# A bank of the score pool for the first of a tile's four transposed halves

## The chip, the cores and the metric

The kernel runs on one core of one Trainium2 chip. The metric is the device time of one execution in microseconds (us); three executions of the kernel before took 832.18, 831.68 and 832.12, median 832.12. One more execution was taken by the hardware profiler, and every row below is from it.

## The reference

Three stages follow one another. The change touches the first alone.

```
attention: B=2, H=8, S=768, D=64
  scores = q @ k.T / 8 + bias(head, distance)
  keep   = the first 8 keys, and the 96 latest keys up to the query itself
  a      = softmax(where(keep, scores, -1e9));  x = a @ v        -> 1536 x 512
experts (4): out += p[:, e] * (relu(x @ w1[e]) @ w2[e])
gate:        ((x @ w1) * (x @ w2)) @ w3 @ w_out
```

## The kernel before

The 1536 queries are cut into 12 tiles of 128 (6 for each batch). A loop of 12 turns, here turn 0 to turn 11, computes a tile's attention over a window of 232 keys (96 before, 8 global, 128 of its own; the first tile of a batch, in turns 0 and 1, has only its own 128). The eight heads are handled as two groups of four (`gr` 0 and 1). The order of all instructions on each engine is the order in which the code issues them. It is a software pipeline over three tiles; in the turn of tile `u`, `one_back` is the tile before it and `two_back` the one before that. The steps of a tile:

- scores (line 246, TensorE, called PE in the profile): per group two PSUM tiles `sp` from the pool `ps_s`, which has 4 banks. Per turn that is 8 matmuls in the program, 16 in the trace.
- `least` (line 261, VectorE, DVE): adds the bias and takes the negated row maximum, once per head, so 8 per turn; it is what frees a bank of the scores. A small read of the accumulator follows each.
- `weights` (line 272, ScalarE, ACT): the exponentials and their sums, 8 per turn.
- `inverse_sums` (lines 231, 232, DVE) and `normalize` (line 300, GpSimd, POOL): the weights are multiplied by the inverse of the sums, a run of four products per group.
- `transposes` (line 284, PE): each group of four heads is transposed in two halves, each half (two heads, two blocks of 128 each) into a PSUM tile `tp` from the pool `ps_t`, which has 3 banks. Four halves per tile of queries.
- `copy` (line 291): brings a half to SBUF as `ptT`. Half 0 of a group goes by DVE, half 1 by ACT.
- `values` (lines 323, 324, 326, PE): the product with v, into the one bank `op`, from which `split_x_hi` (line 444, ACT) and `split_x_lo` (line 450, DVE) write the two parts of x.

In a turn the PE does: the scores of `u`, the values of `two_back`, then the four halves of `one_back` (group 0 half 0, group 0 half 1, group 1 half 0, group 1 half 1). The copies of group 0 stand in the same turn, half 1 (ACT, between two exponentials) ahead of half 0 (DVE, behind the eight `least`); those of group 1 stand at the start of the next turn, behind the next scores. With three banks for four halves a turn, the fourth half takes the bank of the half whose copy stands first, group 0 half 1. From turn 6 on, ACT also casts a piece of the first expert's weights in each turn (line 340), and POOL subtracts it (line 341).

Behind the loop a tail finishes the last two tiles between the first matmuls of the experts (`up_ahead`, lines 56 to 58), and the experts and the gate follow, three matmuls for each product.

Of the kernel before, what the change touches and what calls it, by code (L numbers as in the profile page):

```python
# [8 lines left out]
F32 = mybir.dt.float32  # L9
# [9 lines left out]
P = 128  # L19
# [98 lines left out]
def banded_attention(tc, g, x_hi, x_lo, slots, experts):  # L118
    nc = tc.nc
    with ExitStack() as ctx:  # L120
# [7 lines left out]
        ps_s = ctx.enter_context(tc.tile_pool(name="ps_s", bufs=4, space=PSUM))  # L128
        ps_t = ctx.enter_context(tc.tile_pool(name="ps_t", bufs=3, space=PSUM))
# [146 lines left out]
        def transposes(u, gr):  # L276
            pt = st[u][gr]
            tps = []
            for half in range(2):
                tp = ps_t.tile([P, 2, 2, P], F32, name="tp")  # L280
                for hh in range(2):
                    for j in range(2 if u % NQ else 1):
                        c = slice(j * (LW + GW), j * (LW + GW) + P)
                        nc.tensor.transpose(tp[:, hh, j], pt[:, 2 * half + hh, c], g.ident)  # L284
                tps.append(tp)
            st[u][gr] = tps
# [57 lines left out]
        for m, u in enumerate(order):  # L344
# [39 lines left out]
            if m:  # L384
                transposes(one_back, 0)
                for half in (1, 0):
                    copy(one_back, 0, half)
# [11 lines left out]
            if m:  # L399
                transposes(one_back, 1)  # L400
# [11 lines left out]
        for gr in range(2):  # L412
            transposes(last, gr)
            if gr == 0:
                split_x_hi(nc, *outputs(prior))
            for half in range(2):
                copy(last, gr, half)
            if gr == 0:
                split_x_lo(nc, *outputs(prior))
# [878 lines left out]
```

## Time and profile before

| | |
|---|---|
| median of three runs | 832.12 us |
| the profiled execution, its time | 831.56 us |
| its span, first to last instruction | 829.6 us |
| PE busy | 812.8 us (98%), 4003 matmuls |
| DVE / POOL / ACT busy | 504.0 / 316.4 / 284.9 us |
| loop of 12 turns, first scores to the end of the last turn's transposes | 5.71 to 74.6 us |
| granted TensorE clock, mean | 0.998 |

PE is busy nearly throughout, so a whole-span share tells little: what matters is in which stretch PE's idle time lies, and what ended it. Busy time of matmuls is that of overlapping instructions with modelled ends, so the starts are the firmer numbers.

### The profile page before, as it was taken

How to read it: one execution, taken by the hardware profiler on the slowest of the kernel's cores; microseconds unless marked ns; L12 is line 12 of the kernel's file. 1: busy time of each engine (PE TensorE's matmuls, PEld its weight loads, DVE VectorE, ACT ScalarE, POOL GpSimd, SP SyncE). 2: the span in 40 equal slices, each digit the busy share in tenths (PEclk: the TensorE clock that was granted, in tenths of full speed). 3: DMA queues.
4: the chain of work that ended last, by engine and by line, in shares of the span. 5: the costliest groups of instructions: out<-in, count | busy, mean ns of one | idle time of the engine just before them, and what ended most of it. 6: DMA issues, size and time to landing. Idle time of an engine off the chain costs nothing.

```text
span 829.6 us, 11024 instructions
## 1 busy us (share of the span) xinstructions
PE 812.8 (98%) x4003; PEld 669.0 (81%) x4003; DVE 504.0 (61%) x945; ACT 284.9 (34%) x593; POOL 316.4 (38%) x318
## 2 busy tenths in 40 slices
PE   7999999999999999999999999999999999999997
PEld 4778888888888888888888888888788888888875
DVE  6886355557755556778738563665533743887840
ACT  6897321124321214333323321332442332333210
POOL 6686123535356455550344341422380003333300
PEclk9999999999999999999999999999999999999999
DMA  8850242557453556743101101110622210201011
GB/s 265 244 155 12 78 144 86 166 170 245 154 160 109 166 165 216 229 142 108 54 26 52 39 26 64 50 65 30 192 98 93 85 51 25 102 26 52 0 51 55
DMA packets 38132, 88.10 MB, mean 106 GB/s; under 512 B 3690, under 2 KB 9882, under 8 KB 38070
## 3 DMA queue, kind: packets, MB, share of 16 engines
q1 hardware_dynamic: 37398, 86.79, 32.9%
q8 instruction: 33, 0.54, 0.3%
q10 hardware_dynamic: 672, 0.54, 0.3%
q14 instruction: 29, 0.24, 0.1%
HBM read 73.66 MB, written 13.66 MB: 105 GB/s over the span
## 4 chain that ended last, share of the span: by engine, by line
PE 91%; DVE 4%; ACT 3%; DMA 1%; issue 1%; POOL 0%; DVEq 0%; ACTq 0%; POOLq 0%
PE z L56 18%; PE z L58 18%; PE z L57 18%; PE o L56 11%; PE o L58 11%; PE o L57 11%; DVE t L261 2%; ACT pt L272 2%; PE sp L246 1%; PE tp L284 1%; DMA keys<-in_k_dram 1%; ACT xh L444 1%; ACT ptT L291 0%; PE sp L56 0%; PE sp L58 0%
## 5 line engine op out<-in xcount | busy, mean ns | idle before, releaser
L58 PE MATMUL z<-xh,sl 128*128 128x512 f32 x428 | 166.6, 389 | 0.0
L56 PE MATMUL z<-xh,sh 128*128 128x512 f32 x428 | 166.5, 389 | 0.0
L57 PE MATMUL z<-xl,sh 128*128 128x512 f32 x428 | 166.5, 389 | 0.0
L547 POOL TENSOR_TENSOR cr<-cr,cb 128x512 f32<-128x512 f32 x40 | 51.6, 1290 | 126.6 <-issue 118.7
L58 PEld LDWEIGHTS z<-xh,sl 128*128 128x128 f32 x428 | 80.3, 188 | 17.2 <-DVE sl L51 0.2
L57 PEld LDWEIGHTS z<-xl,sh 128*128 128x128 f32 x428 | 80.3, 188 | 16.7
L56 PEld LDWEIGHTS z<-xh,sh 128*128 128x128 f32 x428 | 80.4, 188 | 16.6
L51 POOL TENSOR_TENSOR sl<-wr,sh 128x512 fp32r<-128x512 f32 (+1 forms) x32 | 32.1, 1024 | 148.7 <-ACT sh L50 148.4
L51 DVE TENSOR_TENSOR sl<-wr,sh 128x1024 fp32r<-128x1024 f32 (+1 forms) x57 | 70.3, 1240 | 23.5 <-ACT sh L50 22.7
L801 POOL TENSOR_TENSOR acc<-acc,t 128x512 f32<-128x512 f32 x36 | 49.3, 1403 | 85.1 <-DVE t L800 85.1
L50 ACT CAST sh<-wr 128x1024 fp32r<-128x1024 f32 (+2 forms) x89 | 70.6, 816 | 21.6 <-PE z L57 10.3
L532 POOL TENSOR_SCALAR ca<-ca 128x512 f32<-128x512 f32 x40 | 61.9, 1548 | 26.7 <-ACT ca L530 26.7
L700 DVE TENSOR_TENSOR t<-t,z 128x512 f32<-128x512 f32 x56 | 37.5, 681 | 32.3 <-PE z L58 27.9
L300 POOL TENSOR_TENSOR pt<-pt,r 128x232 f32<-128x232 f32 (+1 forms) x95 | 48.8, 546 | 16.3 <-ACT pt L272 9.6
L56 PE MATMUL z<-sh,sh 128*128 128x512 f32 x128 | 49.9, 390 | 0.8 <-DVE t L800 0.8
L57 PE MATMUL z<-sl,sh 128*128 128x512 f32 x128 | 49.8, 389 | 0.0
L58 PE MATMUL z<-sh,sl 128*128 128x512 f32 x128 | 49.8, 389 | 0.0
L272 ACT ACTIVATE pt<-t,negmax 128x232 f32<-128x232 f32 (+1 forms) x96 | 44.5, 465 | 10.1 <-DVE negmax L261 6.0
L261 DVE CUSTOM_DVE_ANT_0 t<-sp,bias 128x232 f32<-128x232 f32 (+1 forms) x96 | 30.5, 374 | 9.5 <-PE sp L246 9.5
L51 POOL TENSOR_TENSOR sl<-t,sh 128x256 fp32r<-128x256 f32 (+1 forms) x24 | 23.5, 995 | 31.3 <-ACT sh L50 31.1
L56 PE MATMUL o<-h0h,sh 128*128 128x512 f32 x84 | 32.8, 390 | 0.0
L57 PE MATMUL o<-h0l,sh 128*128 128x512 f32 x84 | 32.7, 389 | 0.0
(255 smaller groups left out, 1728.5 us busy)
## 6 DMA issues: line engine op xcount, KB each, us to landing
wr<-in_w_moe_dram SPq DMA_DIRECT2D x44, 512.0 KB, 4.2
raw<-in_w3t_dram SPq DMA_DIRECT2D x16, 512.0 KB, 4.7
raw<-in_w_ab_dram SPq DMA_DIRECT2D x16, 512.0 KB, 4.2
wr<-wab_d SPq DMA_DIRECT2D x16, 512.0 KB, 3.2
raw<-in_w_out_dram SPq DMA_DIRECT2D x8, 512.0 KB, 3.5
w3t_d<-cr SPq DMA_DIRECT2D x16, 256.0 KB, 2.4
wab_d<-cr SPq DMA_DIRECT2D x16, 256.0 KB, 2.2
wr<-w3t_d SPq DMA_DIRECT2D x8, 512.0 KB, 3.3
```

The costliest lines, as they stand in the source:

```text
L50: nc.scalar.copy(hi, src)
L51: (lo_engine or nc.vector).tensor_tensor(lo, src, hi.bitcast(F32), op=ALU.subtract)
L56: nc.tensor.matmul(out, wh, xh, start=start, stop=False)
L57: nc.tensor.matmul(out, wh, xl, start=False, stop=False)
L58: nc.tensor.matmul(out, wl, xh, start=False, stop=stop)
L261: nc.vector.tensor_tensor_reduce(out=t[:, 0:w], in0=st[u]["sp", gr][hh % 2][:, hh // 2, 0:w], in1=bb, scale=-SCALE, scalar=3.0e38, op0=ALU ...
L272: nc.scalar.activation(st[u][gr][:, hh, 0:w], t[:, 0:w], AF.Exp, bias=nm, scale=-1.0, accum_out=st[u]["sums"][:, h : h + 1])
L300: nc.gpsimd.tensor_tensor(pt[:, hh, 0:w], pt[:, hh, 0:w], r[:, hh : hh + 1].to_broadcast([P, w]), op=ALU.mult)
L532: nc.gpsimd.tensor_scalar(a, a, 2.0**-15, None, op0=ALU.max)
L547: nc.gpsimd.tensor_tensor(rest, rest, top.bitcast(F32), op=ALU.add)
L700: add = lambda o, a, b: nc.vector.tensor_tensor(o, a, b, op=ALU.add)
L801: nc.gpsimd.tensor_tensor(acc[c][:, d], acc[c][:, d], t, op=ALU.add)
```

## The change

The tile of group 0, half 0 comes from the pool of the scores, `ps_s`, under their name `sp`; the other three halves stay in `ps_t`, where each then has a bank of its own in every turn. Neither pool grows. The code is called from the same place, and nothing else is edited.

```diff
             for half in range(2):
-                tp = ps_t.tile([P, 2, 2, P], F32, name="tp")
+                first = gr == half == 0
+                tp = (ps_s if first else ps_t).tile([P, 2, 2, P], F32, name="sp" if first else "tp")
                 for hh in range(2):
```

The order of the instructions is the same on every engine; only waits of PE differ. The pool of scores now has five tiles in a turn for four banks, and hands a bank out in the order in which banks come free: the transposed half takes the bank of group 0's first score tile (free after the third `least`), and the next turn's four score tiles take those free after the fourth, the seventh and the eighth `least` and, last, the bank of the transposed half (free after its DVE copy).

The first place is PE in turn 4, before: the four halves `tp_576`, `tp_581`, `tp_599`, `tp_604`, and the score tiles of turn 5, `sp_618` to `sp_628`. In brackets stand the semaphores waited for.

```order
L284 MATMUL tp_576<-ident_63,pt_418 128x128 [waits Pool_49]
...
L284 MATMUL tp_581<-ident_63,pt_418 128x128 [waits PE_49,Pool_49]
...
L284 MATMUL tp_599<-ident_63,pt_425 128x128 [waits Pool_49]
...
L284 MATMUL tp_604<-ident_63,pt_425 128x128 [waits Activation_49,Pool_49]
...
L246 MATMUL sp_618<-keys_96,qr_403 128x232 [waits DMAHW2_49,DMAHW1_49,DVE_49]
```

The fourth half waits for ACT: the copy of the second half, whose bank it takes.

The same rows of the changed kernel, where the first half is `sp_576`:

```order
L285 MATMUL sp_576<-ident_63,pt_418 128x128 [waits DVE_49,Pool_49]
...
L285 MATMUL tp_581<-ident_63,pt_418 128x128 [waits PE_49,Pool_49]
...
L285 MATMUL tp_599<-ident_63,pt_425 128x128 [waits PE_49,Pool_49]
...
L285 MATMUL tp_604<-ident_63,pt_425 128x128 [waits Pool_49]
...
L246 MATMUL sp_618<-keys_96,qr_403 128x232 [waits DMAHW2_49,DMAHW1_49,DVE_49]
```

The wait for ACT is gone from the fourth half, and the first half waits for DVE instead. The third waits for PE itself, that is for its own bank's writes of the turn before.

The second place is PE's values in turn 4, which read the copied halves of the tile two back: before, the second half (`ptT_478`), the third and the fourth.

```order
L323 MATMUL op_557<-ptT_478,va_234 64x128
...
L323 MATMUL op_557<-ptT_526,va_234 64x128 [waits DVE_49]
...
L323 MATMUL op_557<-ptT_528,va_234 64x128 [waits Activation_49]
```

And now:

```order
L324 MATMUL op_557<-ptT_478,va_234 64x128 [waits Activation_49]
...
L324 MATMUL op_557<-ptT_526,va_234 64x128 [waits DVE_49]
...
L324 MATMUL op_557<-ptT_528,va_234 64x128 [waits Activation_49]
```

The wait for the ACT copy of the second half has moved here from the fourth half, to a matmul of the next turn.

## Rows read from the trace of the kernel before

**Rows 1.** Stretches: length, busy us (instructions) of PE, PEld, DVE, ACT, POOL, clock, DMA.
```profile
31.53:74.60 43.07, 40.55 (x449) 34.75 (x449) 34.68 (x161) 39.02 (x140) 34.34 (x62) 1.00 0.46 136
89.20:300.00 210.80, 210.80 (x932) 174.08 (x930) 120.91 (x204) 52.39 (x82) 86.54 (x63) 1.00 0.49 153
```
**Rows 2.** Groups by form, first 150 us: busy us, mean ns, idle before and releasers.
```profile
L284 PE MATMUL tp<-ident,pt 128*128 128x128 f32 x176 | 24.7, 279 | 7.1 <-ACT ptT L291 3.9 <-POOL pt L300 3.2
```
**Rows 3.** Chain that ended last, in turn 7: start us, us, what.
```profile
48.90 0.48 ACT ptT L291
...
49.51 0.63 PE tp L284 x4
```
**Rows 4.** Timeline of PE, turns 4, 7, 11: start us, us, what [idle before].
```profile
30.97 0.63 PE L284 MATMUL tp<-ident,pt 128*128 128x128 f32 x4 [0.36 <-ACT ptT L291]
...
43.89 1.84 PE L246 MATMUL sp<-keys,qr 64*128 64x232 f32 x16
...
47.62 1.53 PE L284 MATMUL tp<-ident,pt 128*128 128x128 f32 x12
49.51 0.63 PE L284 MATMUL tp<-ident,pt 128*128 128x128 f32 x4 [0.36 <-ACT ptT L291]
50.07 1.84 PE L246 MATMUL sp<-keys,qr 64*128 64x232 f32 x16
...
74.23 0.63 PE L284 MATMUL tp<-ident,pt 128*128 128x128 f32 x4 [0.36 <-ACT ptT L291]
```
**Rows 5.** Timeline of DVE, ACT, POOL, turns 7 and 8, and the tail.
```profile
45.48 0.49 ACT L272 ACTIVATE pt<-t,negmax 128x232 f32<-128x232 f32 x1 [0.54 <-POOL pt L300]
...
46.16 2.17 POOL L300 TENSOR_TENSOR pt<-pt,r 128x232 f32<-128x232 f32 x4 [0.71 <-ACT pt L272]
...
46.20 0.08 DVE L261 DVE_READ_ACCUMULATOR2_ANT negmax<- 128x1 f32 x1
...
48.31 0.69 DVE L291 COPY ptT<-tp 128x512 f32<-128x512 f32 x1 [0.43 <-PE tp L284]
...
49.46 2.17 POOL L300 TENSOR_TENSOR pt<-pt,r 128x232 f32<-128x232 f32 x4 [0.43 <-ACT ptT L291]
...
49.78 0.68 DVE L291 COPY ptT<-tp 128x512 f32<-128x512 f32 x1
...
50.71 0.41 ACT L340 CAST sh<-wr 128x256 fp32r<-128x256 f32 x1
51.15 0.40 DVE L261 CUSTOM_DVE_ANT_0 t<-sp,bias 128x232 f32<-128x232 f32 x1 [0.69 <-PE sp L246]
...
74.18 3.80 POOL L300 TENSOR_TENSOR pt<-pt,r 128x232 f32<-128x232 f32 x7 [0.44 <-ACT ptT L291]
```
**Rows 6.** Timeline of POOL, PE and DVE, turns 1 to 4.
```profile
9.30 2.97 POOL L300 TENSOR_TENSOR pt<-pt,r 128x128 f32<-128x128 f32 x8 [0.55 <-ACT pt L272]
...
13.30 1.84 PE L246 MATMUL sp<-keys,qr 64*128 64x232 f32 x16
...
15.66 1.47 POOL L300 TENSOR_TENSOR pt<-pt,r 128x128 f32<-128x128 f32 x4 [1.53 <-ACT pt L272]
...
18.19 2.17 POOL L300 TENSOR_TENSOR pt<-pt,r 128x232 f32<-128x232 f32 x4 [1.06 <-DVE r L232]
...
18.59 0.41 DVE L291 COPY ptT<-tp 128x256 f32<-128x256 f32 x1
...
19.17 1.84 PE L246 MATMUL sp<-keys,qr 64*128 64x232 f32 x16
...
20.25 0.40 DVE L261 CUSTOM_DVE_ANT_0 t<-sp,bias 128x232 f32<-128x232 f32 x1 [1.26 <-PE sp L246]
...
21.44 2.17 POOL L300 TENSOR_TENSOR pt<-pt,r 128x232 f32<-128x232 f32 x4 [1.08 <-ACT pt L272]
...
25.35 1.84 PE L246 MATMUL sp<-keys,qr 64*128 64x232 f32 x16
```
**Rows 7.** Timeline of PE, the last tile's transposes in the tail.
```profile
79.54 2.16 PE L284 MATMUL tp<-ident,pt 128*128 128x128 f32 x16
```

## The prediction

> **What bounds the kernel now.** I read the busy time by stretches first. From 89.2 to 300 us PE is busy for all of 210.80 us, at a granted clock of 1.00: the experts are bound by PE alone, and whatever starts them earlier ends the kernel earlier by as much. In the steady part of the attention loop, 31.53 to 74.60 us (seven turns), PE is busy for 40.55 of 43.07 us, also at 1.00 [rows 1]. So 2.5 us are idle there, seven times 0.36.
>
> The groups say what it is: the transposes wait 7.1 us in the loop, 3.9 of it for `ptT` of ACT and 3.2 put down to `pt` of POOL [rows 2]. The chain that ended last has the same link: the ACT copy 48.90 + 0.48 = 49.38, then the last four transposes at 49.51, a hand-over of 0.13 [rows 3]. The timeline of PE shows the place: twelve transposes at 47.62, then a stop of 0.36, then four, then the next turn's scores at 50.07. The same stop ends turn 4 at 30.97 and turn 11 at 74.23, eight times in all [rows 4]. A turn lasts 50.07 - 43.89 = 6.18 us.
>
> The stop costs more than its idle column says. Twelve transposes last 1.53 us and one 0.279 [rows 2, 4], so they start (1.53 - 0.279) / 11 = 0.114 us apart, the thirteenth could have started at 47.62 + 12 x 0.114 = 48.98, and it starts at 49.51: **0.53 us**. The Trainium skill ("Perfetto Trace Analysis", section "Identifying the Most-Contended Engine") says that matmul busy time measures badly because matmuls are pipelined; by the idle column the eight stops would be worth 8 x 0.36 = 2.9 us, by starts 8 x 0.53 = 4.2. I go by the starts.
>
> **The change, part by part.** *The wait removed in turns 4 to 11.* The fourth half's bank is free since the turn before, so it follows the third at once, if its weights are normalised: POOL's run of four ends at 46.16 + 2.17 = 48.33 [rows 5], 0.65 ahead of 48.98. PE then needs 6.18 - 0.53 = 5.65 us a turn. Whether the others can follow:
> - ACT goes from its first exponential at 45.48 to the end of its cast at 50.71 + 0.41 = 51.12, so 5.64 us, with no idle row between.
> - DVE: the copy of the first half starts 48.31 - 43.89 = 4.42 after the scores, the second copy ends 49.78 + 0.68 - 48.31 = 2.15 later, and the next `least` is due 51.15 - 50.07 = 1.08 after the next scores. The turn can't be shorter than 4.42 + 2.15 - 1.08 = 5.49.
> - POOL: the second run ends 49.46 + 2.17 - 43.89 = 7.74 after the scores, the first of the next turn is due 46.16 - 43.89 = 2.27 after its scores: 5.47 [rows 4, 5].
>
> All four fit in 5.65, with PE the last by a hair. Eight turns: 8 x 0.53 = 4.24 us.
>
> *Turns 1 to 3.* Here the same wait goes, and POOL is late next. A scores start follows the last transposes by 50.07 - 49.51 - 3 x 0.114 = 0.22.
> - Turn 1: POOL's products end at 9.30 + 2.97 = 12.27, the last transpose starts 0.13 later, turn 2's scores at 12.62 instead of 13.30: 0.68.
> - Turn 2: its products end at 15.66 + 1.47 - 0.68 = 16.45, so turn 3's scores start at 16.45 + 0.13 + 0.22 = 16.80 instead of 19.17: 2.37 by now. (The groups put 3.2 us of the transposes' idle time down to POOL. In this turn POOL's fourth product ended at 17.13, 2 us ahead of the scores, so it was another engine that PE waited for, and what the last transposes waited for besides is the ACT copy.)
> - Turn 3: DVE is behind now. Its second copy ends at 18.59 + 0.41 - 0.68 = 18.32, later than 16.80 + 1.08, so the first `least` moves from 20.25 to 18.32. POOL's second run would move with it from 21.44 to 19.51 but its first run ends at 18.19 + 2.17 - 0.68 = 19.68; from there 2.17 to 21.85. The last two transposes start 0.13 later, the scores 0.22 + 0.11 behind that: 22.31 instead of 25.35 [rows 6].
>
> So 3.04 us by turn 4. This part isn't shown as directly: it is at least the 0.68 of turn 1, at most 3.04. I take 3.04, because each step ends at a row.
>
> *Tail.* The last tile's 16 transposes take 2.16 us; unbroken they would take 0.279 + 15 x 0.114 = 1.99 [rows 2, 7]: 0.17.
>
> *Waits added.* The first half waits for the third `least`, whose read ends at 46.20 + 0.08, 1.34 before the transposes at 47.62 [rows 4, 5]. Behind it in PE's queue stand all other transposes and the next scores, so its cover matters: gone, it would cost its lateness in each turn. The next scores wait for `least` four, seven and eight and for the first half's copy, which ends at 48.31 + 0.69 = 49.00, against 49.54 for the first scores of the shorter turn, and the fourth bank is written later still. The wait in the values for the ACT copy comes a turn after that copy. All at nothing. The wait instruction itself, one more ahead of the first transposes, is not shown; its nearest row is the twelve transposes, with such a wait inside them and no gap: zero. The other end: as much as the hand-over of 0.13 in each of 11 turns, 1.4 us. Below nothing it can't be, since PE gains nothing by an instruction more.
>
> Sum: 4.24 + 3.04 + 0.17 = 7.45 us. The profiled execution, 831.56 (a span of 829.6 and 2.0 around it), becomes 824.1. The median of the runs is 0.56 above it, so **824.7 us** there.
>
> **Rivals.**
> 1. *Another engine becomes the bound, and a part is given back.* For it: ACT's 5.64 is within 0.01 of PE's 5.65, DVE and POOL within 0.2, and in turns 3 to 5 DVE and ACT are behind PE. Against: in turns 4 and 5 ACT has no cast. Should the turn stop at 5.9, the sum is 8 x 0.28 + 3.04 + 0.17 = 5.45, 826.7; should only turn 1 gain early on, 4.24 + 0.68 + 0.17 = 5.1, 827.0; both 3.1, 829.0. One way to it would be DVE and POOL slowing each other as they overlap more. The rows speak against: four products take 2.17 between DVE's instructions, 0.543 each, and seven take 3.80 in the tail, also 0.543 [rows 5]. The Trainium skill ("SBUF — State Buffer", section "Who interferes with whom") has a price for it where a DVE instruction reads two inputs from SBUF while GpSimd reads it; the trace shows none here.
> 2. *The change doesn't do what it says for the time:* the fourth half still starts at 49.51 for another reason that ends there, and nothing moves: 832.1. For it speaks that the idle row before the exponentials and those of the transposes name POOL too; against it, that POOL's products are over at 48.33.
> 3. *Slower: the DVE copy holds the scores.* Their fourth bank is now freed by a copy that DVE does behind eight `least`. It decides once the copy ends later than that bank is wanted: in the turn of 6.18 that is 50.07 + 10 x 0.115 (ten of the sixteen matmuls of 1.84 us) = 51.2, 2.2 after 49.00. Were the copy 2.5 late, each of 11 turns would cost 0.3 more than before: 835.4. Nothing in the rows makes it so late; the loop had 0.43 of idle right before it [rows 5].
>
> **How the numbers follow.** My forecast (6 to 8.5 us gained) 0.62; rival 1 (2 to 6 us) 0.28; no change 0.06; slower 0.04. 0.2% of 832 is 1.7 us, about what a measurement can tell from nothing. Faster is the first two, 0.90; same 0.06; slower 0.04. The likeliest case alone spans 823.6 to 826.1; to leave out no more than 2 in 10 the range takes in rival 1 down to 3.9 us, so 823.6 to 828.2.
>
> **What would show it.** Right: in turns 4 to 11 sixteen transposes without a stop, and scores that start 5.65 us apart; turn 4's scores near 22.3 and the last turn's transposes over near 67.2 instead of 74.6; the experts' stretch moved as a whole and no longer. If the turns are at 5.8 or more, the row of what PE waits for names the engine of rival 1; if PE stops ahead of its first transposes or its scores, for DVE, it is rival 3. Wrong altogether: an unchanged stop of 0.36 before the fourth half.

## The result and the profile after

The changed kernel's median is 824.66 us (823.10 to 825.47, six executions) against 831.79 for the kernel before in the same call: a ratio of 0.9911, 95% interval 0.9898 to 0.9924. It is faster, and 824.7 was forecast. Of all executions below one, with ten warm-up matmuls, took 1019.99 us at a mean granted clock of 0.753, and it is left out.

In the steady turns the stop before the fourth half [rows 4] is gone. The timeline of PE of the changed kernel, from turn 8 on (start us, us, what), with all lines one further down in the code:

```profile
46.40 1.84 PE L246 MATMUL sp<-keys,qr 64*128 64x232 f32 x16
...
50.13 0.66 PE L285 MATMUL sp<-ident,pt 128*128 128x128 f32 x4
50.62 1.47 PE L285 MATMUL tp<-ident,pt 128*128 128x128 f32 x12
52.02 1.84 PE L246 MATMUL sp<-keys,qr 64*128 64x232 f32 x16
```

The sixteen transposes run without an idle row, now as four under the scores' name and twelve under their own. A turn lasts 52.02 - 46.40 = 5.62 to 5.63 us instead of 6.18. The transposes start 50.13 - 46.40 = 3.73 after the scores, and before it was 47.62 - 43.89 = 3.73 too [rows 4]: the wait for `least` that now stands ahead of them costs nothing.

The stretches of it show the same (length, busy us and instructions of PE, PEld, DVE, ACT, POOL, clock, DMA); the first runs from turn 5's scores to the first matmul of `up_ahead` and answers to the first of [rows 1], the second is the experts':

```profile
29.52:68.73 39.21, 39.21 (x449) 34.89 (x449) 36.09 (x162) 39.16 (x141) 34.42 (x62) 1.00 0.52 155
83.06:300.00 216.94, 216.94 (x959) 179.32 (x958) 123.94 (x209) 52.85 (x83) 91.65 (x67) 1.00 0.49 156
```

PE was idle for 2.5 us there and is never idle now. ACT is busy for 39.16 of 39.21 us as well, which says by itself that one of the two is the bound and not which; an experiment below tells them apart.

The groups of the transposes in the first 150 us (busy us, mean ns, idle before), which answer to [rows 2]:

```profile
L285 PE MATMUL tp<-ident,pt 128*128 128x128 f32 x132 | 17.5, 276 | 0.2
L285 PE MATMUL sp<-ident,pt 128*128 128x128 f32 x44 | 7.3, 286 | 0.3 <-DVE negmax L261 0.3
```

and what PE waited for between 5 and 90 us (us, times, longest):

```profile
PE sp L246 <- DMA keys<-in_k_dram: 0.8, 1, 0.8
PE sp L285 <- DVE negmax L261: 0.3, 1, 0.3
PE op L327 <- ACT ptT L292: 0.2, 1, 0.2
```

Of 7.1 us of idle time ahead of the transposes 0.5 is left, and the new wait for DVE shows once, in turn 3.

Where the time came from, by starts on PE. One execution of each kernel is a thin base here, because the very beginning differs from one execution to the next; a later profile of the changed kernel began nearly as the one of before did, and stands in the last column. (One between the two, of 825.32 us, began late as well: turn 1's scores at 9.74, then 13.52, 44.85 and 14.31 for the next three rows.)

| stretch | before | changed | gain forecast | changed, later profile |
|---|---|---|---|---|
| start to turn 1's scores | 8.20 | 10.22 | 0 | 7.96 |
| turn 1 to turn 4 | 17.15 | 13.67 | 3.04 | 14.01 |
| turn 4 to the first `up_ahead` | 49.26 | 44.84 | 4.24 | 44.84 |
| from there to the experts' first `o` | 14.56 | 14.33 | 0.17 | 14.32 |
| the rest of the span | 740.43 | 740.44 | 0 | 739.77 |

The change is worth 3.14 + 4.42 + 0.24 = **7.80 us** for nearly the same start (forecast 7.45). In the first profile 1.7 of it are missing: turn 1 began 2.02 later, and turns 1 to 3, 0.34 shorter than in the later profile, gave that much back. The last row says nothing about the change: in the fourteen profiles of this case, of all kernels, the rest of the span lies between 739.5 and 741.1 us, the changed kernel's among them at 740.44, 740.88 and 739.77.

### The profile page after: what moved, and what is told of

It is laid out like the page before. It is cut to its first block, busy times and chain, and to the rows that moved or that the text cites. A ratio compares the mean times of both kernels' runs of the same rounds, so it can differ in the third digit from the quotient of the medians.

```text
span 823.5 us, 11032 instructions
## 1 busy us (share of the span) xinstructions
PE 813.5 (99%) x4002; PEld 670.3 (81%) x4003; DVE 505.1 (61%) x945; ACT 283.9 (34%) x593; POOL 316.4 (38%) x318
## 4 chain that ended last, share of the span: by engine, by line
PE 96%; ACT 1%; DVE 1%; DMA 1%; issue 0%; POOL 0%; ACTq 0%; DVEq 0%
PE z L56 18%; PE z L57 18%; PE z L58 18%; PE o L58 11%; PE o L56 11%; PE o L57 11%; PE sp L246 2%; PE tp L285 1%; PE op L324 1%; PE op L325 1%; ACT pt L272 1%; PE sp L285 1%; DMA keys<-in_k_dram 1%; PE sp L56 0%; PE sp L58 0%
```

## The experiments

All were timed beside the kernel before. Its medians in the four calls were 830.95, 832.18, 832.18 and 831.48, so each ratio counts against its own call, and the stretches of the profiles carry what is below 1 us.

**Is it the number of banks?** The changed kernel with one bank fewer for the transposes, so the other three halves share two:

```diff
-        ps_t = ctx.enter_context(tc.tile_pool(name="ps_t", bufs=3, space=PSUM))
+        ps_t = ctx.enter_context(tc.tile_pool(name="ps_t", bufs=2, space=PSUM))
```

> The changed kernel, but the pool of the transposed halves has two banks in place of three; the first half still lies in a bank of the scores, and the order is the same. The fourth half of a turn then takes the bank of the second half again and waits for its ACT copy, as in the kernel before. Theory (that one wait is what costs): everything else of the change is there, yet the stop before the fourth half is back in turns 1 to 11, a turn lasts 6.18 us, and the time is that of before, 831.8 +- 0.7. Rival (the gain comes from the scores' and halves' other banks or from the fifth tile in the pool of scores, not from this wait): turns of 5.63, about 824.7.

832.22 us, ratio 1.001 (0.9999 to 1.002). The stop is back; PE's timeline of this kernel:

```profile
47.41 0.66 PE L285 MATMUL sp<-ident,pt 128*128 128x128 f32 x4
47.90 1.04 PE L285 MATMUL tp<-ident,pt 128*128 128x128 f32 x8
49.30 0.63 PE L285 MATMUL tp<-ident,pt 128*128 128x128 f32 x4 [0.36 <-ACT ptT L292]
49.86 1.84 PE L246 MATMUL sp<-keys,qr 64*128 64x232 f32 x16
```

A turn is 6.18 again (43.68 to 49.86). The whole gain is thus that the fourth half doesn't take a bank that ACT's copy must first empty; that the first half lies in another pool gives nothing by itself.

**Are the terms separate?** The change in turns 1 to 3 alone, and in turns 4 to 11 and the tail alone:

```diff
-                first = gr == half == 0
+                first = share and gr == half == 0
...
-                transposes(one_back, 0)
+                transposes(one_back, 0, m < 4)
```

> The change in turns 1 to 3 alone; from turn 4 on and in the tail all four halves lie in the three banks as before. Theory: the turns from 4 on last 6.18 us again, and what is gained is the early part, which my working put at 3.04 and the profile of the changed kernel shows as 1.46 at turn 4's scores with a start that came 2.0 later: 2.5 to 3.5 us by the clock of equal starts, 828.3 to 829.3. Rival (only turn 1's 0.68 is gained, the rest is lost to POOL and DVE): 831.1.

> The change in turns 4 to 11 and in the tail alone; turns 1 to 3 as before. Theory: eight turns at 5.63 in place of 6.18 and the tail's 0.2: 4.4 + 0.2 = 4.6 us, 827.2. By the idle column of the trace of before (eight stops of 0.36) it would be 2.9 + 0.2, 828.7. Rival (another engine takes over as soon as the turns get short, and the early lead is what hides it): turns of 5.8 or more, 828.5 to 830.

Turns 1 to 3 alone: 828.19 us, ratio 0.9963 (0.9950 to 0.9977). Turns 4 to 11 and the tail: 827.78, ratio 0.9956 (0.9942 to 0.9970); its six times lie in two groups, 826.48 to 827.03 and 828.54 to 828.73, on either side of the 827.2 expected, so the stretches of the profile say more than this median. In the profile of the first, turn 1 to turn 4 takes 13.99 instead of 17.15, a gain of 3.16. But turn 4 then lasts 6.74 (PE, and ACT's copy of the second half):

```profile
22.01 1.84 PE L246 MATMUL sp<-keys,qr 64*128 64x232 f32 x16
25.74 1.53 PE L285 MATMUL tp<-ident,pt 128*128 128x128 f32 x12
27.46 0.58 ACT L292 COPY ptT<-tp 128x512 f32<-128x512 f32 x1
28.19 0.63 PE L285 MATMUL tp<-ident,pt 128*128 128x128 f32 x4 [0.92 <-POOL pt L301]
28.75 1.84 PE L246 MATMUL sp<-keys,qr 64*128 64x232 f32 x16
```

With the shared bank ACT's copy is waited for again, and ACT is behind by then: its copy runs at 27.46 for 0.58, and the fourth half starts 0.15 behind it (the row names POOL, whose products of that half were long done). So 0.57 of the 3.16 is given back where the bank is shared, and none where it isn't. In the profile of the second, turn 4 to `up_ahead` takes 44.84 and the tail 14.33, gains of 4.42 and 0.23, as with the whole change. Apart the two gain 2.59 + 4.65 = 7.24, together 7.80, and the difference is what turn 4 gave back.

**The changed kernel again.**

> The changed kernel once more, unchanged, for a second profile and more times. Theory: 824.7 again; the profile of the first look had its first matmuls 0.457 us apart up to 10.2 us, where the profile of before had 0.245 from 6.8 us on, so turn 1 started at 10.22 in place of 8.20 there. If that is chance, a second look may show turn 1 at 8.2, turn 4 near 22.3 and a time near 823; times spread over 2 us. If the change causes it, the second look has the late start as well.

> The changed kernel once more, beside the next one in the same call: 822.9 to 825.5, both paces of the start among its runs, median near 823.5 to 824.5.

823.18 us (ratio 0.9898, 0.9882 to 0.9913) and 824.67 us (0.9913, 0.9900 to 0.9926). Of 15 executions of this kernel seven lie between 822.88 and 823.47 and eight between 824.48 and 825.47, nothing between. The rows of the beginning tell the two apart. The changed kernel's first profile (825.47 us):

```profile
5.54 2.08 PE L246 MATMUL sp<-keys,qr 64*128 64x128 f32 x16 [0.78 <-DMA keys<-in_k_dram]
7.55 2.74 PE L172 MATMUL tp<-warm 128*128 128x512 bf16 x6
10.22 1.30 PE L246 MATMUL sp<-keys,qr 64*128 64x128 f32 x16
```

and the later one (822.92 us), with POOL's products of turn 3:

```profile
5.47 1.16 PE L246 MATMUL sp<-keys,qr 64*128 64x128 f32 x16 [0.70 <-DMA keys<-in_k_dram]
6.56 1.47 PE L172 MATMUL tp<-warm 128*128 128x512 bf16 x6
7.96 1.43 PE L246 MATMUL sp<-keys,qr 64*128 64x128 f32 x16
...
12.36 1.84 PE L246 MATMUL sp<-keys,qr 64*128 64x232 f32 x16
...
16.51 1.84 PE L246 MATMUL sp<-keys,qr 64*128 64x232 f32 x16
...
17.25 4.30 POOL L301 TENSOR_TENSOR pt<-pt,r 128x232 f32<-128x232 f32 x8 [1.05 <-DVE r L232]
...
21.97 1.84 PE L246 MATMUL sp<-keys,qr 64*128 64x232 f32 x16
```

The same six matmuls take 2.74 us in one and 1.47 in the other, the last one's length included; from start to start they are 0.43 and 0.215 us apart. PE's program is the same in the kernel before up to there, and the changed kernel shows both paces, so the change by itself doesn't bring the slow one. Whether the kernel before has it too isn't shown: its times spread as widely (830.6 to 833.5 in one call), but its one profile has the quick pace. Nor does a time alone tell the pace, as the rest of the span varies by 1.5 us: one of 824.32 us, with ten warm-up matmuls, began quickly.

**Is ACT the bound already?** The changed kernel with ACT's cast of a piece of weights issued twice in turns 6 to 11, and, as the same function serves there, for three larger pieces in the tail (0.62 us each):

```diff
             nc.scalar.copy(hi, raw)
+            nc.scalar.copy(hi, raw)
```

> The changed kernel with ACT's cast of a piece of weights issued twice in turns 6 to 11: 0.31 to 0.41 us more of ACT in each of six turns, the values written are the same. Theory (PE sets the turn of 5.63, ACT has a slack that its full idle column hides: its cast waits for nothing and is wanted late): at most 1.0 us longer, since about 1 us of lag is swallowed before the transposes or the values wait for ACT. Rival 1 of the prediction in its sharp form (ACT's 5.64 is the bound of the turn already): every added part shows, 6 x 0.31 to 6 x 0.41 = 1.9 to 2.5 us longer, and turns of 5.95 to 6.05 from turn 6 on.

824.10 us (823.41 to 825.12), ratio 0.9906 (0.9891 to 0.9921): not told apart from the changed kernel. ACT's timeline of this kernel, the two casts of a turn and the exponential behind them, and the first cast of the next two turns:

```profile
46.68 0.41 ACT L341 CAST sh<-wr 128x256 fp32r<-128x256 f32 x1
47.12 0.41 ACT L342 CAST sh<-wr 128x256 fp32r<-128x256 f32 x1
47.43 0.49 ACT L272 ACTIVATE pt<-t,negmax 128x232 f32<-128x232 f32 x1
...
52.64 0.41 ACT L341 CAST sh<-wr 128x256 fp32r<-128x256 f32 x1
...
58.61 0.41 ACT L341 CAST sh<-wr 128x256 fp32r<-128x256 f32 x1
```

ACT's turn is 5.96 here, PE's is 5.63 (39.07, 44.70, 50.32, 55.95 in its timeline). ACT falls back by 0.33 a turn, some 2.0 us in six turns, and PE's turns stay at 5.63 until the last: turn 4 to `up_ahead` is 45.01 instead of 44.84, where the last two transposes of turn 11 waited. The tail, with its three more casts, is 14.52 instead of 14.33. So 0.36 shows of more than 2 us. PE is the bound, and ACT's full column doesn't show how far ACT may fall behind before PE waits: six turns of 0.33 hardly use that up. That a longer loop would is argued, not run. The second cast adds 0.44 from start to start (46.68 to 47.12), so ACT's own work is 5.96 - 0.44 = 5.52 us a turn, 0.11 below PE's.

**Does it matter which half?** The fourth half in the score pool instead of the first, then the third:

```diff
-                first = gr == half == 0
+                first = gr == half == 1
```

> The changed kernel, but the fourth half (group 1, half 1) goes to the score pool instead of the first. Each other half again has a bank of its own, so the stop before the fourth half should be gone as well; but the scores' fourth bank is now freed by ACT's copy of the fourth half, at the start of the next turn. In the changed kernel's steady turns that copy ends 1.3 to 1.4 us after the scores start (47.13 + 0.57 against 46.40), a hand-over of 0.13 makes it 1.4 to 1.55, and the fourth bank is wanted ten matmuls in, at 1.15: PE would stop 0.3 to 0.4. Theory (once PE has stopped, ACT lies nearer to PE, and with 5.64 a turn it doesn't fall back): 0.3 to 1.0 us slower than the changed kernel in all, turns of 5.63 to 5.66. Rival (rival 3's sense: the stop repeats in each turn): 8 x 0.3 to 8 x 0.4, so 2.4 to 3.2 us slower, turns of 5.95. Second rival (any half does as well): the same time and no stop in the scores.

828.97 us, ratio 0.9957 (0.9944 to 0.9971): by the ratios about 4 us behind the changed kernel. My theory fell, and the rival's size was short too. The timeline of PE, its weight loads and ACT in this kernel:

```profile
47.39 1.53 PE L285 MATMUL tp<-ident,pt 128*128 128x128 f32 x12
...
48.52 0.58 ACT L292 COPY ptT<-tp 128x512 f32<-128x512 f32 x1
...
49.29 2.34 PE L246 MATMUL sp<-keys,qr 64*128 64x232 f32 x16
...
49.96 0.57 ACT L292 COPY ptT<-sp 128x512 f32<-128x512 f32 x1
...
50.58 0.69 PEld L246 LDWEIGHTS sp<-keys,qr 64*128 64x128 f32 x6 [0.21 <-ACT ptT L292]
...
53.52 1.53 PE L285 MATMUL tp<-ident,pt 128*128 128x128 f32 x12
```

The scores take 2.34 instead of 1.84 in each turn, a turn is 6.13, and 8 x 0.50 with 0.9 more in turns 1 to 3 are the 4.9 us by which `up_ahead` starts later here (73.64) than in the changed kernel's first profile (68.73). PE's busy column is full all the same (42.75 of 42.75 us from turn 5 to `up_ahead`): the stop lies inside the matmuls. I had thought ACT would catch up after one stop. It can't, because its copy of the second half waits for the transposes of the same turn, and the copy of the fourth stands two exponentials behind it. That is a ring. The transposes start at 47.39; 1.13 later the copy of the second half starts; 2.01 later the copy of the fourth ends, at 50.53; PE's weight loads go on at 50.58; 2.94 later the next transposes start at 53.52. In all 1.13 + 2.01 + 0.05 + 2.94 = 6.13. (From transposes to transposes the sum must give the turn; what counts is that the links follow each other closely: the second half's last transpose ends at 47.39 + 7 x 0.114 + 0.279 = 48.47, 0.05 ahead of its copy.)

> The third half (group 1, half 0) in the score pool instead of the first. What the run with the fourth half showed: its turns were 6.13, because the scores' fourth bank waited for ACT's copy (49.96 + 0.57 = 50.53, the scores began at 49.29 and want that bank 1.15 later, at 50.44), and that copy stands behind ACT's copy of the second half, which waits for the transposes of the same turn: a ring PE, ACT, PE. Theory now (what counts is when the bank's last reader ends against 1.15 after the scores' start, and through which engine the ring closes): the third half's reader is DVE's copy at 46.66 + 0.60 = 47.26 in the changed kernel, where the scores began at 46.40 and want the bank at 47.55; some 0.15 to 0.3 of slack, the ring doesn't bind, turns of 5.63 to 5.70 and a time within 0.6 us of the changed kernel in the same call. Rival (any half whose copy stands in the next turn stops the scores): turns near 6.1, 4 to 5 us slower, as with the fourth half.

826.19 us, ratio 0.9932 (0.9921 to 0.9944); turns of 5.84, between the two numbers expected. The timeline of PE and DVE in this kernel, in turns 3 and 8:

```profile
19.03 0.41 DVE L292 COPY ptT<-sp 128x256 f32<-128x256 f32 x1
...
19.50 1.05 PE L246 MATMUL sp<-keys,qr 64*128 64x232 f32 x6 [0.46 <-DVE ptT L292]
...
45.21 1.09 PE L285 MATMUL tp<-ident,pt 128*128 128x128 f32 x8
...
45.91 0.69 DVE L292 COPY ptT<-tp 128x512 f32<-128x512 f32 x1 [0.41 <-PE tp L285]
...
47.11 2.05 PE L246 MATMUL sp<-keys,qr 64*128 64x232 f32 x16
...
47.37 0.68 DVE L292 COPY ptT<-sp 128x512 f32<-128x512 f32 x1
...
51.05 1.09 PE L285 MATMUL tp<-ident,pt 128*128 128x128 f32 x8
```

The ring again, now through DVE. The transposes start at 45.21, the copy of the first half 0.70 later, the copy of the third ends 2.14 behind that, at 48.05; taking 0.06 of hand-over (in turn 3 the copy ends at 19.44 and PE goes on at 19.50) the next transposes at 51.05 come 2.94 later: 5.84. What I had wrong is when the bank is wanted. The scores start at 47.11 and last 0.21 too long, so it was wanted at 48.11 - 0.21 - 47.11 = 0.79 after their start; with the fourth half it is 50.58 - 0.50 - 49.29 = 0.79 as well. I had put 1.15, from sixteen matmuls at even distances, and had taken 0.60 for a copy that lasts 0.68 (46.66 to 47.34 in the changed kernel).

For the change as it was made the ring starts with the transposes at 50.13 and goes through DVE's copy of the first half:

```profile
50.82 0.69 DVE L292 COPY ptT<-sp 128x512 f32<-128x512 f32 x1 [0.19 <-PE sp L285]
```

It ends at 51.51; with 0.06 + 2.94 the ring is 4.38 us. The turn is the longer of the ring and PE's own 5.63: 5.63, 5.84 and 6.13 for the first, the third and the fourth half. The rule fits the three runs from which its links are read; no run was forecast by it.

**The start.** Eleven, nine and ten warm-up matmuls instead of eight, to fill PE's idle time ahead of the keys:

```diff
-WARM = 8
+WARM = 11
```

> Eleven warm-up matmuls instead of eight, else the changed kernel. In the changed kernel's profile PE idles 0.74 to 1.05 us before turn 0's scores, for the keys' DMA, and then its first matmuls step 0.457 us until about 10 us; in the kernel before they step 0.245 from 6.8 us on. Theory A (the idle ahead of the scores decides which of the two paces follows): no idle row ahead of turn 0's scores, turn 1's scores near 8.0, and the slower start is gone: all runs near 822.9. Theory B (the pace has nothing to do with that idle): the same two kinds of start as in the changed kernel, times between 822.9 and 825.4. If the three added matmuls are themselves longer than the wait for the keys, turn 0's scores start later by the rest, at most 3 x 0.46 = 1.4 us.

> Nine warm-up matmuls. With eleven, PE had no idle ahead of turn 0's scores and all four times lay within 0.5 us (824.05 to 824.58), but the scores started at 6.08 instead of 5.49. One more matmul, some 0.43 us, ends at about 5.2, ahead of the keys: turn 0's scores at 5.5, an idle row of about 0.3 us. If an idle of 0.3 already brings the slow pace of the first matmuls, times spread from 822.9 to 825.4 as in the changed kernel; if not, all are near 822.9 to 823.5.

> Ten warm-up matmuls: they end at about 5.65, just behind the keys (5.49 to 5.54). No idle row ahead of turn 0's scores, which start 0.15 later than with eight. If the idle brings the slow pace: no slow start, all times within 0.5 us, near 823.3 to 823.8. If not: the spread of the changed kernel, 822.9 to 825.4.

> Nine warm-up matmuls once more. If the ninth keeps the first matmuls from the slow pace (none of four runs was above 824.6): all runs 822.6 to 823.6, 0.3 to 1.2 below the changed kernel's median. If that was chance: the changed kernel's spread, and no difference.

Eleven: 824.51 us (ratio 0.9906), all within 0.53, but turn 0's scores start at 6.08 and turn 1's at 9.04, where theory A wanted 8.0; and turn 0's scores take 1.63 us in place of the 1.16 of the quick pace, so they began slowly even without idle time ahead of them. Ten: 823.24 to 824.32 in four executions (0.9897, 0.9882 to 0.9913). Nine: 823.46 and 823.06 (0.9898 and 0.9903, the second 0.9889 to 0.9917). Beside the last stood the changed kernel with 0.9913 (0.9900 to 0.9926), and the intervals overlap. Of eight executions with nine matmuls two were at 824.6; of 15 with eight, eight were above 824.4. That may be chance, so I don't call it a better kernel. The idle time isn't the cause by itself: it is 0.71 to 0.78 us in the four profiles that kept the slow pace beyond 9 us (all with eight warm-up matmuls), but two others with eight have 0.70 and 0.73 at the quick pace, and one with nine has 0.83.

## Why the prediction was right

- *The stop counted by starts, 0.53 a turn.* Right: 6.18 - 5.63 = 0.55, and eight of them 4.42 against 4.24 forecast. The idle column would have given 2.9. The bank run shows that nothing else is in it.
- *PE the last by a hair, ACT 0.01 behind.* Right as to the bound, and rival 1 is out: no turn from turn 4 on is above 5.63, and ACT with 0.33 more a turn lengthened only the last, by 0.17. The hair was too thin, though: ACT's own work is 5.52, not 5.64, because the forecast took the cast at its length of 0.41, where the next instruction starts 0.31 behind it (47.12 to 47.43); and an engine that runs behind without being waited for has slack besides.
- *Turns 1 to 3, 3.04.* Right for the same start. From turn 1's scores on, turn 2's, 3's and 4's came after 4.40, 8.55 and 14.01 us; forecast were 4.42, 8.60 and 14.11. In the first profile the later start hid this. There POOL's second run in turn 3 waited for the sums from ACT's exponentials, which the forecast had not reckoned with; with the equal start POOL's eight products ran in one piece to 17.25 + 4.30 = 21.55, 13.59 after turn 1's scores (forecast 13.65).
- *The tail, 0.17.* It gave 0.24.
- *The waits added, nothing.* Right: 3.73 us from the scores to the transposes, before and after. A stop of about 0.3 put down to DVE shows in turn 3 of the first profile and in turn 1 of the later one, but POOL's products ended behind it (at 23.47 and 12.04) and set the next scores' start (23.89 and 12.36). The fourth bank of the scores is wanted 0.79 after they start, earlier than the ten matmuls at 0.115 of rival 3, but the copy of the first half ends 1.25 ahead of that still (the ring of 4.38 against 5.63). Rival 3's mechanism is real, though: it is what cost 0.21 and 0.50 a turn when the third or the fourth half took the bank.
- *The level.* The forecast agrees with the median to 0.1 us, which is partly luck: 0.35 of gain were missed, and the changed kernel's executions fall on either side of a gap from 823.47 to 824.48, of which the median of six happened to take the upper side.

## What to carry to other kernels

When two users share a ring of buffers, give the borrowed buffer to the one whose last reader ends earliest before the next need; add up the ring from the writer through the reader's queue back to the writer, and the turn is the longer of that ring and the busiest engine's own work. Three runs here fit that rule. Take the price of a stop from starts, not from the idle column. An engine's full busy column doesn't make it the bound: ask who waits for it, and for how many turns it can fall behind before somebody does.

## What the runs showed of the hardware

TensorE starts every execution slowly, and when it speeds up differs with the same program. In all fourteen profiles the first warm-up matmuls (128x512) start 0.43 us apart; later ones start 0.215 apart, a ratio of 2.0 like that of its two clock levels, 1.2 and 2.4 GHz. The trace also holds entries of the granted clock. The first, at 1.00, begins at 10.55 us in the changed kernel's first profile and at 5.11 in the later one; over all profiles it begins at 3.96 to 5.28 us in nine, at 7.10 with eleven warm-up matmuls and at 9.22 to 10.57 in four. Matmuls ahead of that entry have the slow pace and those behind it the quick one, so it is the clock that rises there. (The views print 1.00 from the start, because nothing is recorded ahead of the first entry.) In the four late profiles PE had by then done its eight warm-up matmuls, a pause of 0.71 to 0.78, turn 0's sixteen scores and at least five more warm-up matmuls. A late rise put turn 1's scores 1.8 to 2.3 us later in the changed kernel, and turns 1 to 3 gave 0.3 to 0.5 of that back. What decides when the clock rises stays open.

The sixteen scores don't start at even distances but in pairs, mostly 0.20 us apart: in the changed kernel, from 46.40 on, eight have started by 47.28 and ten by 47.30. So the first matmul of the fourth bank starts 0.89 us after the scores do, and not 1.15. A stop also costs a little more than the wait: behind the one that ends at 50.58 with the fourth half, the next pair starts 0.30 later and not 0.20, and the load of its weights starts together with the stopped matmul instead of 0.19 ahead. The 0.89 less this 0.10 is the 0.79 at which the bank was wanted.
